# Attention and FFN on one core: the side work of the first FFN pass issued at other steps

## The chip, the cores and the metric

The kernel runs as one program on 1 core of one Trainium2 chip. The metric is the time of one execution in device microseconds (us). Below, PE is the matrix engine (TensorE), PEld its weight loads, DVE is VectorE, ACT is ScalarE, POOL is GpSimd and SP is SyncE, whose queue issues nearly all DMAs. Every engine works through its own queue in order and waits at an instruction whose inputs or buffers are not ready.

## The reference

```python
# attention: q, k, v are (4, 8, 768, 64)
mask = q_bucket[:, :, :, None] == k_bucket[:, :, None, :]
scores = np.where(mask, scale * q @ k.T, -1e9)
attn_out = softmax(scores) @ v
# FFN over x = (3072 tokens, 512)
h = x @ w_in                       # 512 x 2048
g = np.where(h >= 1, h, np.where(h <= -1, 0.0, (h + 1) ** 2 / 4))
return (g @ w_out).astype(np.float32)   # 2048 x 512
```

## The kernel before

The program has two phases: attention over 32 heads, then the FFN. Every float32 operand of a matrix product is split in two: a high part, rounded to the PE's fast format by a copy (a CAST in the trace), and a low part, the difference (a subtraction on line L39). A product of two such operands is three matmuls: high by high, high by low, low by high.

The FFN (`ffn`, L568) works through the 3072 tokens in 8 chunks of 384, and for each chunk through 16 tiles of 128 of the hidden dimension. One pair of chunk c and hidden tile f is a **step**. The loop at L669 runs over the steps in the order of `ffn_order`: steps 0 to 7 are (0,0) to (0,7), then chunk 1 and chunk 0 alternate ((1,0) is step 8, (0,8) step 9, and so on) until step 31; chunks 2 to 7 follow. This first pass over two chunks takes place while output weights and chunk 1's input are still being made.

A step issues in this order:

- the jobs of `prep[n]`, a table of what else is due at step n (L670);
- `g_lo` (L623): on DVE, the low part `glo` (L627) of the activation of the step before last;
- `gemm1` (L593): 12 matmuls (L600) into one of two PSUM buffers `h`: for each of the four input tiles ct = 0 to 3 high weight by high x, high weight by low x, low weight by high x. Low x of tile ct is so read by matmul 2, 5, 8 and 11. Then ACT makes `t` (L605) and `z` (L606), and DVE finishes the activation (L607, L608). L607 writes `t` in place, so it waits until L606 has read it;
- `g_hi` (L615): on ACT, the high part `ghi` (L620) of the step before;
- `gemm2` (L631) of three steps earlier (`GLAG` = 3): 9 matmuls (L638), for each of three token tiles `ghi` by high weight, `ghi` by low weight, `glo` by high weight.

So ACT and DVE have one queue each for the activations and for the jobs of `prep`, in the order in which the loop issues them. The jobs of the first pass are:

- **Chunk 1's input** (`xm.make`, L541, four tiles, four parts each): part 0 (L547) and part 1 (L550) on DVE scale the tile, part 2 (L552) rounds it on ACT, part 3 (L39) makes its low part on DVE. The tiles lie in buffers `xraw`, `xraw`, `xe`, `xr`.
- **Staged output weights**, hidden tiles 2 to 5: split earlier, parked in DRAM, and now fetched by a DMA (L102, `get`), rounded on ACT (L87, `s5`) and subtracted on DVE (L39, `s6`).
- **The other output weights**, hidden tiles 6 to 15: a DMA of the raw data (L62, `s0`), a square on ACT with a DVE operation (L69, L70, `s1`), DVE operations (L74, L78, L82, `s2` to `s4`), the rounding on ACT (L87, `s5`) and the subtraction on DVE (L39, `s6`).

`lsh_attn_ffn` sets the steps of the weights at L792 to L801. `need` is the step at which gemm2 first reads the tile; the numbers subtracted from it are the lead of s0 to s6. `wraw` and `wsq`, which these jobs fill, have two buffers each, so the DMA of a tile waits on SP until the tile two before it has been read.

```python
670  for fn, a in prep.pop(n, ()):
671      fn(*a)
672  g_lo()
673  pend.append((c, f, gemm1(c, f)))
674  g_hi(1)
675  if len(pend) > GLAG:
676      gemm2(*pend.pop(0))
```

Of the kernel before, what the change touches and what calls it, by code (L numbers as in the profile page):

```python
# [29 lines left out]
NFT = DFF // P  # L30
# [526 lines left out]
def ffn_order():  # L557


    steps = [(0, f) for f in range(LEAD)]  # L560
    for f in range(NFT):
        steps.append((1, f))
        if f + LEAD < NFT:
            steps.append((0, f + LEAD))
    return steps + [(c, f) for c in range(2, NCH) for f in range(NFT)]


def ffn(ctx, tc, wih, wil, woh, wol, xm, xa, xb, out, prep):  # L568
    nc = tc.nc
    xp = ctx.enter_context(tc.tile_pool(name="xp", bufs=1, reuse_waits="tile"))  # L570
    gp = ctx.enter_context(tc.tile_pool(name="gp", bufs=2, reuse_waits="tile"))
    ps_h = ctx.enter_context(tc.tile_pool(name="ps_h", bufs=2, space=PSUM, reuse_waits="tile"))
    ps_y = ctx.enter_context(tc.tile_pool(name="ps_y", bufs=6, space=PSUM, reuse_waits="tile"))
    mh = xp.tile([P, 1], F32, name="mh")
    nc.vector.memset(mh, 0.5)
    m1 = xp.tile([P, 1], F32, name="m1")
    nc.vector.memset(m1, -1.0)
    xc = (xp.tile([P, NCT, CH], F32R, name="xhi"), xp.tile([P, NCT, CH], F32R, name="xlo"))
    xs = [xa, xb] + [xc, xa] * ((NCH - 2) // 2)

    def piece(name):
        return xp.tile([P, CH], F32, name=name, bufs=2)

    def load_x(c, ct):
        if ct == 0:
            xm.load_sv(c, xp.tile([P, NCT, 2], F32, name="xsv"))
        if c == 1:
            xm.load_raw(c, ct, piece(("xraw", "xraw", "xe", "xr")[ct]))
        else:
            xm.load_raw(c, ct, piece("xraw"))  # L590
            xm.load_er(c, ct, piece("xe"), piece("xr"))

    def gemm1(c, f):  # L593
        hi, lo = xs[c]
        ps = ps_h.tile([P, 512], F32, name="h")
        n = 0
        for ct in range(NCT):
            cs = slice(ct * P, (ct + 1) * P)
            for w, x in ((wih[f], hi), (wih[f], lo), (wil[f], hi)):
                nc.tensor.matmul(out=ps[:, 0:CH], lhsT=w[:, cs], rhs=x[:, ct, :], start=(n == 0),  # L600
                                 stop=(n == 3 * NCT - 1))
                n += 1
        t = gp.tile([P, CH], F32, name="t")
        z = gp.tile([P, CH], F32, name="z", bufs=3)
        nc.scalar.activation(out=t, in_=ps[:, 0:CH], func=AF.Relu, scale=0.5, bias=mh)  # L605
        nc.scalar.activation(out=z, in_=t, func=AF.Relu, scale=1.0, bias=m1)  # L606
        nc.vector.scalar_tensor_tensor(out=t, in0=t, scalar=1.0, in1=t, op0=ALU.min, op1=ALU.mult)  # L607
        nc.vector.tensor_tensor(out=z, in0=t, in1=z, op=ALU.add)  # L608
        g = [None, None, z]
        to_hi.append(g)  # L610
        return g

    to_hi, to_lo = [], []

    def g_hi(left):  # L615

        while len(to_hi) > left:
            g = to_hi.pop(0)
            g[0] = gp.tile([P, CH], F32R, name="ghi", bufs=GLAG)
            nc.scalar.copy(out=g[0], in_=g[2])  # L620
            to_lo.append(g)

    def g_lo():  # L623
        while to_lo:
            g = to_lo.pop(0)
            g[1] = gp.tile([P, CH], F32R, name="glo", bufs=GLAG)
            nc.vector.tensor_tensor(out=g[1], in0=g[2], in1=g[0].bitcast(F32), op=ALU.subtract)  # L627

    ys = {}

    def gemm2(c, f, g):  # L631
        ghi, glo, _ = g
        if f == 0:
            ys[c] = [ps_y.tile([P, 512], F32, name="y") for _ in range(CH // P)]
        for m in range(CH // P):
            ms = slice(m * P, (m + 1) * P)
            for k, (g_, w) in enumerate(((ghi, woh[f]), (ghi, wol[f]), (glo, woh[f]))):
                nc.tensor.matmul(out=ys[c][m], lhsT=g_[:, ms], rhs=w, start=(f == 0 and k == 0),  # L638
                                 stop=(f == NFT - 1 and k == 2))
            if f == NFT - 1:  # L640
                r0 = c * CH + m * P
                if c == NCH - 1 and m == CH // P - 1:
                    for n, cp in ((0, nc.vector.tensor_copy), (1, nc.scalar.copy)):
                        cs = slice(n * DM // 2, (n + 1) * DM // 2)
                        ot = piece(("xraw", "xe")[n])[:, 0:DM // 2]
                        cp(out=ot, in_=ys[c][m][:, cs])
                        nc.sync.dma_start(out=out[r0:r0 + P, cs], in_=ot)
                    continue
                ot = xp.tile([P, DM], F32, name="ot", bufs=2)
                nc.scalar.copy(out=ot, in_=ys[c][m])  # L650
                nc.sync.dma_start(out=out[r0:r0 + P, :], in_=ot)

    def at(n, fn, *a):
        prep[n].append((fn, a))

    at(2 * NFT + 1, lambda: xm.sums_load(*(piece(n)[:, 0:NF] for n in ("xe", "xr")), B - 1))
    at(2 * NFT + 4, xm.sums_add)
    at(2 * NFT + 4, xm.sums_inv, B - 1)
    for ct in reversed(range(NCT)):
        prep[0].insert(0, (load_x, (1, ct)))  # L660
    for c in range(1, NCH):
        for ct in range(NCT):
            if c > 1:
                at((c - 1) * NFT + 4 + 2 * ct, load_x, c, ct)
            for part in range(4):
                n = (1, 2, 4, 5)[ct] + (0, 0, 1, 2)[part] if c == 1 else (c - 1) * NFT + 6 + 2 * ct + part
                at(n, xm.make, c, ct, part, *xs[c], [nc.vector if c == 1 else nc.gpsimd] * 2)
    pend = []
    for n, (c, f) in enumerate(ffn_order()):  # L669
        for fn, a in prep.pop(n, ()):  # L670
            fn(*a)
        g_lo()
        pend.append((c, f, gemm1(c, f)))
        g_hi(1)
        if len(pend) > GLAG:
            gemm2(*pend.pop(0))
    g_hi(0)
    g_lo()
    while pend:
        gemm2(*pend.pop(0))  # L680
# [3 lines left out]
def lsh_attn_ffn(ctx: ExitStack, tc: tile.TileContext, qk, v, pj, cv, w_in, w_out, out):  # L684
    nc = tc.nc
# [9 lines left out]
    NSTG = 10  # L695
    wih = [wp.tile([P, DM], F32R, name=f"wih{i}") for i in range(NW1)]
    wil = [wp.tile([P, DM], F32R, name=f"wil{i}") for i in range(NW1)]

    r_d = [xdp.tile([H, S], F32, name=f"rd{b}") for b in range(B)]
    xm = XMaker(nc, x_d, s_d, e_d, r_d)  # L700

    def flat(t):
        return t.rearrange("p a b s -> p (a b s)")
# [8 lines left out]
    for hi, lo in w0[0:4]:  # L712
# [3 lines left out]
    xa, xb = (tuple(flat(t)[:, n * NCT * CH:(n + 1) * NCT * CH].rearrange("p (c n) -> p c n", c=NCT)  # L716
                    for n in range(2)) for t in (T2[i0], T2[i1]))
# [3 lines left out]
    ws = WeightSplit(nc, wst, DM)  # L721

    tasks = defaultdict(list)
    prep = defaultdict(list)

    def at(g, fn, *a):
        tasks[g].append((fn, a))
# [8 lines left out]
    def wo_steps(i, cp, stage=None, low=None):  # L736
        return ws.steps(wout_v[i], (P, DM, 2), woh[i], wol[i], cp, stage, low)

    woh = [hi for hi, lo in wo]
    wol = [lo for hi, lo in wo]  # L740
# [3 lines left out]
    late = {}  # L744
    for n in range(NSTG):
        stage = xdp.tile([P, DM], F32, name=f"wd{n}")
        i = n - (NFT - NW1)
# [44 lines left out]
    for i in range(2, NFT):  # L792
        n = i + NFT - NW1
        need = i + GLAG if i < LEAD else 2 * i + GLAG + 1 - LEAD
        if n < NSTG:
            st = zip(late[n], (i - 4, i - 2, i - 1))
        else:
            st = zip(wo_steps(i, nc.scalar, None, nc.vector), (need - m for m in (9, 5, 5, 4, 4, 3, 2)))
        for fn, m in st:
            if m >= 0:  # L800
                prep[m].append((fn, ()))  # L801
    ffn(ctx, tc, wih, wil, woh, wol, xm, xa, xb, out, prep)


def _consts():
# [47 lines left out]
```

## Time and profile before

| what | value |
|---|---|
| median of 3 runs | 1021.6 us (1021.07 to 1022.53) |
| the profiled execution | 1021.61 us, span 1019.6 us |
| PE busy | 993.9 us, 97% of the span |
| DVE busy | 696.6 us, 68% |
| ACT busy | 647.5 us, 64% |
| POOL busy | 395.0 us, 39% |

The profile is of one execution. Its span runs from the first instruction to the last; the execution's own time is 2.0 us longer. Matmuls overlap, so the time from the start of one to the start of the next tells more than the duration of one. The FFN's first matmul starts at 473.54 us of the span.

### The profile page before, as it was taken

To read this page: it belongs to the slowest core of one execution; us is meant where nothing else is said; L and a number is where in the kernel's file an instruction comes from. 1 tells how busy PE (TensorE), PEld (TensorE's weight loads), DVE (VectorE), ACT (ScalarE), POOL (GpSimd) and SP (SyncE) were. 2 spreads that over 40 slices of the span, in tenths; PEclk is the share of its full clock that TensorE was granted. 3 is DMA by queue.
4 is the path that set the end of the run, shared out by engine and by line. 5 is a ranking of instruction groups with operands and counts; after the bars stand their busy time and mean duration, and the time that the engine had idled before them with its cause. 6 is when DMAs were issued, how large, how long until landed. Compare 5 with 4: busy or idle time off the path is not lost.

```text
span 1019.6 us, 15241 instructions
## 1 busy us (share of the span) xinstructions
PE 993.9 (97%) x5180; PEld 917.5 (90%) x5180; DVE 696.6 (68%) x1108; ACT 647.5 (64%) x1430; POOL 395.0 (39%) x458
## 2 busy tenths in 40 slices
PE   5899999999999999999999999999999999999998
PEld 4789999999999999989799999999999999999997
DVE  7678999999999998786977644544535445345332
ACT  5779888998899989886655444444444444444433
POOL 6666777777887777563000210201202102012000
PEclk9999999999999999999999999999999999999999
DMA  2645666766665655546222102102021021020000
GB/s 89 167 110 155 160 171 174 182 169 169 158 171 153 152 141 144 127 107 180 63 80 88 50 32 79 47 22 81 24 77 48 1 79 47 32 71 24 32 1 32
DMA packets 52229, 99.06 MB, mean 97 GB/s; under 512 B 12856, under 2 KB 33976, under 8 KB 52152
## 3 DMA queue, kind: packets, MB, share of 16 engines
q1 hardware_dynamic: 51936, 98.09, 35.9%
q8 instruction: 41, 0.67, 0.3%
q14 instruction: 36, 0.29, 0.1%
q10 hardware_dynamic: 216, 0.00, 0.0%
HBM read 57.38 MB, written 15.52 MB: 71 GB/s over the span
## 4 chain that ended last, share of the span: by engine, by line
PE 89%; DVE 5%; ACT 2%; DMA 1%; issue 1%; SPq 0%; POOL 0%; DVEq 0%; ACTq 0%
PE y L638 26%; PE h L600 25%; PE smax L258 7%; PE o L332 6%; PE s L298 6%; PE o L330 6%; PE o L331 6%; PE s L297 6%; PE o L178 2%; DVE nm L262 1%; DMA wsq<-wd 1%; DVE nm L359 1%; DVE pl L39 0%; ACT ph L306 0%; DMA pj_raw<-in_pj_dram 0%
## 5 line engine op out<-in xcount | busy, mean ns | idle before, releaser
L607 DVE SCALAR_TENSOR_TENSOR t<-t 128x384 f32<-128x384 f32 x128 | 73.0, 571 | 257.6 <-ACT z L606 257.5
L605 ACT ACTIVATE t<-h,mh 128x384 f32<-128x384 f32 x128 | 74.3, 581 | 267.4 <-PE h L600 266.2
L306 ACT ACTIVATE ph<-s 128x384 fp32r<-128x384 f32 x380 | 188.1, 495 | 46.9 <-PE s L298 40.6
L262 DVE TENSOR_REDUCE nm<-smax 128x1 f32<-128x768 f32 x186 | 176.2, 947 | 19.9 <-PE smax L258 18.4
L39 POOL TENSOR_TENSOR pl<-pf,ph 128x384 fp32r<-128x384 f32 x128 | 137.9, 1083 | 81.2 <-ACT pf L311 80.8
L39 DVE TENSOR_TENSOR pl<-s,ph 128x384 fp32r<-128x384 f32 x256 | 135.5, 544 | 15.3 <-ACT s L311 14.0
L550 POOL TENSOR_TENSOR xraw<-xraw,xr 128x384 f32<-128x384 f32 x24 | 30.2, 1258 | 272.2 <-DVE xraw L547 272.2
L297 PE MATMUL s<-t 128*128 128x384 f32 x384 | 132.0, 344 | 0.8 <-DVE t L212 0.8
L332 PE MATMUL o<-pl,va 128*128 128x386 f32 x384 | 130.4, 339 | 0.4 <-DVE pl L39 0.3
L298 PE MATMUL s<-t 128*128 128x384 f32 x384 | 130.2, 339 | 0.0
L330 PE MATMUL o<-ph,va 128*128 128x386 f32 x384 | 130.1, 339 | 0.0
L331 PE MATMUL o<-ph,vb 128*128 128x386 f32 x384 | 129.5, 337 | 0.0
L311 ACT ACTIVATE s<-s 128x384 f32<-128x384 f32 x252 | 125.3, 497 | 0.0
L600 PE MATMUL h<-t,wih 128*128 128x384 f32 x480 | 122.7, 336 | 0.0
L638 PE MATMUL y<-t,ghi 128*128 128x512 f32 x384 | 120.2, 394 | 0.0
L258 PE MATMUL smax<-t 128*128 128x384 f32 x372 | 101.5, 353 | 5.4 <-DVE nm L262 4.5
L600 PEld LDWEIGHTS h<-t,wih 128*128 128x128 f32 x480 | 88.0, 188 | 4.9
L258 PEld LDWEIGHTS smax<-t 128*128 128x128 f32 x372 | 63.9, 188 | 22.1 <-DVE nm L262 21.1
L606 ACT ACTIVATE z<-t,m 128x384 f32<-128x384 f32 x128 | 79.0, 617 | 4.1
L638 PEld LDWEIGHTS y<-t,ghi 128*128 128x128 f32 x384 | 71.4, 188 | 11.2
L600 PE MATMUL h<-t,wil 128*128 128x384 f32 x240 | 80.8, 337 | 0.0
L638 PE MATMUL y<-t,glo 128*128 128x512 f32 x192 | 76.3, 398 | 2.9 <-DVE glo L627 2.9
(130 smaller groups left out, 2117.2 us busy)
## 6 DMA issues: line engine op xcount, KB each, us to landing
t<-t SPq DMA_DIRECT2D x60, 384.0 KB
raw<-in_qk_dram SPq DMA_DIRECT2D x15, 768.0 KB
wraw<-in_w_in_dram SPq DMA_DIRECT2D x16, 512.0 KB
wraw<-in_w_out_dram SPq DMA_DIRECT2D x16, 512.0 KB
xd<-xs SPq DMA_DIRECT2D x32, 192.5 KB
vraw<-in_v_dram SPq DMA_DIRECT2D x16, 384.0 KB
out_dram<-ot SPq DMA_DIRECT2D x23, 256.0 KB
xraw<-xd SPq DMA_DIRECT2D x26, 192.0 KB
```

What stands on the lines that cost most here:

```text
L39: eng.tensor_tensor(out=out, in0=a, in1=b, op=ALU.subtract)
L258: nc.tensor.matmul(out=smax[hd][:, hf, 0:HS], lhsT=t2[:, 0, h, i * P:(i + 1) * P], rhs=t2[:, 1, h, hf * HS:(hf + 1) * HS], start=True, sto ...
L262: nc.vector.tensor_reduce(out=nmp(hd)[:, i:i + 1], in_=smax[hd][:, :, 0:HS], axis=AX.XY, op=ALU.max, negate=True)
L297: nc.tensor.matmul(out=ps[:, 0:HS], lhsT=t1[:, 1, h, ks], rhs=t1[:, 0, h, sl], start=True, stop=False)
L298: nc.tensor.matmul(out=ps[:, 0:HS], lhsT=t2[:, 1, h, ks], rhs=t2[:, 0, h, sl], start=False, stop=True)
L306: nc.scalar.activation(out=ph[:, 0:HS], in_=ps[:, 0:HS], func=AF.Exp, scale=SCALE)
L311: nc.scalar.activation(out=pf, in_=ps[:, 0:HS], func=AF.Exp, scale=SCALE)
L330: nc.tensor.matmul(out=o, lhsT=wa, rhs=ph, start=(jj == 0), stop=False)
L331: nc.tensor.matmul(out=o, lhsT=wb, rhs=ph, start=False, stop=False)
L332: nc.tensor.matmul(out=o, lhsT=wa, rhs=pl, start=False, stop=(jj == NJ - 1))
L600: nc.tensor.matmul(out=ps[:, 0:CH], lhsT=w[:, cs], rhs=x[:, ct, :], start=(n == 0), stop=(n == 3 * NCT - 1))
L638: nc.tensor.matmul(out=ys[c][m], lhsT=g_[:, ms], rhs=w, start=(f == 0 and k == 0), stop=(f == NFT - 1 and k == 2))
```

## The change

The change edits only when jobs of the first pass are issued. A second table, `post`, holds jobs that are issued after g_hi, so behind the step's activations, and before gemm2. `g_lo` now comes ahead of the jobs of `prep`. Chunk 1's input is made one step later, its rounding (part 2) in `post` of the same step as parts 0 and 1, its low part two steps after. The roundings of all output weights go to `post`. The staged tiles 2 to 5 are fetched, rounded and subtracted later (tiles 2 and 3 were fetched during attention and still are); tiles 6 to 15 get their steps s1 to s5 one step later or in `post`, and from tile 8 on their DMA three steps later.

```diff
     pend = []
     for n, (c, f) in enumerate(ffn_order()):
+        g_lo()
         for fn, a in prep.pop(n, ()):
             fn(*a)
-        g_lo()
         pend.append((c, f, gemm1(c, f)))
         g_hi(1)
+        for fn, a in post.pop(n, ()):
+            fn(*a)
         if len(pend) > GLAG:
             gemm2(*pend.pop(0))
...
             for part in range(4):
-                n = (1, 2, 4, 5)[ct] + (0, 0, 1, 2)[part] if c == 1 else (c - 1) * NFT + 6 + 2 * ct + part
-                at(n, xm.make, c, ct, part, *xs[c], [nc.vector if c == 1 else nc.gpsimd] * 2)
+                if c == 1:
+                    n = (2, 3, 5, 6)[ct] + (0, 0, 0, 2)[part]
+                    (post if part == 2 else prep)[n].append((xm.make, (c, ct, part, *xs[c], [nc.vector] * 2)))
+                else:
+                    at((c - 1) * NFT + 6 + 2 * ct + part, xm.make, c, ct, part, *xs[c], [nc.gpsimd] * 2)
...
         if n < NSTG:
-            st = zip(late[n], (i - 4, i - 2, i - 1))
+            st = zip(late[n], (i - 1, i - (i < 4), i + 1))
         else:
-            st = zip(wo_steps(i, nc.scalar, None, nc.vector), (need - m for m in (9, 5, 5, 4, 4, 3, 2)))
-        for fn, m in st:
-            if m >= 0:
+            st = zip(wo_steps(i, nc.scalar, None, nc.vector), (need - m for m in (9 if i < 8 else 6, 4, 4, 3, 3, 3, 2)))
+        *st, (cast, m_cast), low = st
+        post[m_cast].append((cast, ()))
+        for fn, m in st + [low]:
+            if n >= NSTG or i > 3 or fn is low[0]:
                 prep[m].append((fn, ()))
```

The instructions are the same, in another order on DVE, ACT and SP. PE's order is the same.

DVE from L608 of step 0 on, before (names are result <- inputs; `t1_0_74<-wsq` are the low parts of output weights 2 and 3, `xraw` is chunk 1's input, tiles 0 and 1):

```order
L608 TENSOR_TENSOR z_6069<-t_6068,z_6069 128x384
L39 TENSOR_TENSOR t1_0_74<-wsq_5929,t1_0_74 128x512
L547 SCALAR_TENSOR_TENSOR xraw_6042<-t2_2_79,xsv_6040,xraw_6042 128x384
L550 TENSOR_TENSOR xraw_6042<-xraw_6042,t2_2_79 128x384
L607 SCALAR_TENSOR_TENSOR t_6095<-t_6095 128x384
L608 TENSOR_TENSOR z_6096<-t_6095,z_6096 128x384
L39 TENSOR_TENSOR t1_0_74<-wsq_5949,t1_0_74 128x512
L547 SCALAR_TENSOR_TENSOR xraw_6044<-t2_2_79,xsv_6040,xraw_6044 128x384
L550 TENSOR_TENSOR xraw_6044<-xraw_6044,t2_2_79 128x384
L627 TENSOR_TENSOR glo_6108<-z_6069,ghi_6101 128x384
```

and with the change:

```order
L608 TENSOR_TENSOR z_6066<-t_6065,z_6066 128x384
L607 SCALAR_TENSOR_TENSOR t_6086<-t_6086 128x384
L608 TENSOR_TENSOR z_6087<-t_6086,z_6087 128x384
L627 TENSOR_TENSOR glo_6095<-z_6066,ghi_6092 128x384
L547 SCALAR_TENSOR_TENSOR xraw_6042<-t2_2_79,xsv_6040,xraw_6042 128x384
L550 TENSOR_TENSOR xraw_6042<-xraw_6042,t2_2_79 128x384
L607 SCALAR_TENSOR_TENSOR t_6112<-t_6112 128x384
L608 TENSOR_TENSOR z_6113<-t_6112,z_6113 128x384
L627 TENSOR_TENSOR glo_6122<-z_6087,ghi_6118 128x384
L39 TENSOR_TENSOR t1_0_74<-wsq_5929,t1_0_74 128x512
```

The first `glo` stood behind six jobs and one more activation; now it stands behind one activation.

DVE before, from L607 of step 6 on (`t2_0_77<-wsq` are the low parts of output weights 6 and 7, `t2_2_79<-xr` is the low part of chunk 1's tile 3, which matmul 11 of step 8 reads; `wa` is a step of output weight 8):

```order
L607 SCALAR_TENSOR_TENSOR t_6277<-t_6277 128x384
L608 TENSOR_TENSOR z_6278<-t_6277,z_6278 128x384
L39 TENSOR_TENSOR t2_0_77<-wsq_6173,t2_0_77 128x512
L70 TENSOR_SCALAR wa_6297<-wraw_6133 128x512
L74 SCALAR_TENSOR_TENSOR wa_6297<-wraw_6133,wsc_111,wa_6297 128x512
L39 TENSOR_TENSOR t2_2_79<-xr_6048,t2_2_79 128x384
L627 TENSOR_TENSOR glo_6304<-z_6241,ghi_6283 128x384
L607 SCALAR_TENSOR_TENSOR t_6319<-t_6319 128x384
L608 TENSOR_TENSOR z_6320<-t_6319,z_6320 128x384
L39 TENSOR_TENSOR t2_0_77<-wsq_6215,t2_0_77 128x512
```

and with the change, from L39 of tile 2 (`xe`) on; the L607 here is step 7's:

```order
L39 TENSOR_TENSOR t2_2_79<-xe_6046,t2_2_79 128x384
L607 SCALAR_TENSOR_TENSOR t_6308<-t_6308 128x384
L608 TENSOR_TENSOR z_6309<-t_6308,z_6309 128x384
L627 TENSOR_TENSOR glo_6326<-z_6271,ghi_6314 128x384
L39 TENSOR_TENSOR t2_0_77<-wsq_6248,t2_0_77 128x512
L70 TENSOR_SCALAR wa_6330<-wraw_6253 128x512
L74 SCALAR_TENSOR_TENSOR wa_6330<-wraw_6253,wsc_111,wa_6330 128x512
L39 TENSOR_TENSOR t2_2_79<-xr_6048,t2_2_79 128x384
L607 SCALAR_TENSOR_TENSOR t_6350<-t_6350 128x384
```

The low part of tile 3 stood ahead of L607 and L608 of step 7; now it stands behind them, behind one more pair of `glo`, and behind output weight 7's subtraction.

ACT, from the last copy of attention on, before (`t1_0_74<-wsq` and `t2_0_77<-wsq` are the roundings of output weights 2, 3, 4 and 5):

```order
L338 COPY xs_5961<-o1_143 128x386
L87 CAST t1_0_74<-wsq_5929 128x512
L605 ACTIVATE t_6068<-h_6055,mh_6034 128x384
L606 ACTIVATE z_6069<-t_6068,m1_6036 128x384
L87 CAST t1_0_74<-wsq_5949 128x512
L605 ACTIVATE t_6095<-h_6082,mh_6034 128x384
L606 ACTIVATE z_6096<-t_6095,m1_6036 128x384
L620 CAST ghi_6101<-z_6069 128x384
L87 CAST t1_0_74<-wsq_6051 128x512
L552 CAST t2_2_79<-xraw_6042 128x384
L605 ACTIVATE t_6123<-h_6110,mh_6034 128x384
```

and with the change:

```order
L338 COPY xs_5961<-o1_143 128x386
L605 ACTIVATE t_6065<-h_6052,mh_6034 128x384
L606 ACTIVATE z_6066<-t_6065,m1_6036 128x384
L605 ACTIVATE t_6086<-h_6073,mh_6034 128x384
L606 ACTIVATE z_6087<-t_6086,m1_6036 128x384
L620 CAST ghi_6092<-z_6066 128x384
L87 CAST t1_0_74<-wsq_5929 128x512
L605 ACTIVATE t_6112<-h_6099,mh_6034 128x384
L606 ACTIVATE z_6113<-t_6112,m1_6036 128x384
L620 CAST ghi_6118<-z_6087 128x384
L87 CAST t1_0_74<-wsq_5949 128x512
L552 CAST t2_2_79<-xraw_6042 128x384
```

The activations of steps 1 and 2 now stand ahead of the roundings of weights 2 and 3; that of weight 4, whose data come by a DMA issued in this pass, moved from ahead of step 2's activation to behind step 4's.

## Rows read from the trace of the kernel before

**Rows 1.** The page's first part: busy time of each engine.

```profile
PE 993.9 (97%) x5180; PEld 917.5 (90%) x5180; DVE 696.6 (68%) x1108; ACT 647.5 (64%) x1430; POOL 395.0 (39%) x458
```

**Rows 2.** Waits in the FFN, engine and line, for whom: total us, times, longest.

```profile
PEld y L638 <- DVE glo L627: 4.7, 4, 1.3
...
PE y L638 <- DVE glo L627: 2.9, 4, 0.9
```

**Rows 3.** PE in order of time: start us, us, engine, line, operation, [idle before].

```profile
481.89 0.63 PE L638 MATMUL y<-t,ghi 128*128 128x512 f32 x2
...
498.81 0.50 PE L638 MATMUL y<-t,glo 128*128 128x512 f32 x1 [0.82 <-DVE glo L627]
...
502.64 0.62 PE L638 MATMUL y<-t,ghi 128*128 128x512 f32 x2
...
505.80 0.51 PE L600 MATMUL h<-t,wih 128*128 128x384 f32 x2
...
506.32 0.51 PE L600 MATMUL h<-t,wih 128*128 128x384 f32 x2
506.67 0.34 PE L600 MATMUL h<-t,wil 128*128 128x384 f32 x1
506.84 0.62 PE L638 MATMUL y<-t,ghi 128*128 128x512 f32 x2
```

**Rows 4.** DVE in order of time, in the FFN's first pass.

```profile
477.24 0.56 DVE L607 SCALAR_TENSOR_TENSOR t<-t 128x384 f32<-128x384 f32 x1 [4.62 <-ACT z L606]
...
489.61 0.68 DVE L39 TENSOR_TENSOR t<-wsq,t 128x512 fp32r<-128x512 f32 x1
490.21 0.42 DVE L70 TENSOR_SCALAR wa<-wraw 128x512 int32<-128x512 int32 x1
490.66 0.75 DVE L74 SCALAR_TENSOR_TENSOR wa<-wraw,wsc,wa 128x512 int32<-128x512 int32 x1
491.33 0.55 DVE L39 TENSOR_TENSOR t<-xraw,t 128x384 fp32r<-128x384 f32 x1
491.81 0.61 DVE L547 SCALAR_TENSOR_TENSOR xe<-t,xsv,xe 128x384 f32<-128x384 f32 x1
492.45 0.56 DVE L550 TENSOR_TENSOR xe<-xe,t 128x384 f32<-128x384 f32 x1
492.93 0.55 DVE L627 TENSOR_TENSOR glo<-z,ghi 128x384 fp32r<-128x384 f32 x1
493.39 0.55 DVE L607 SCALAR_TENSOR_TENSOR t<-t 128x384 f32<-128x384 f32 x1
493.98 0.56 DVE L608 TENSOR_TENSOR z<-t,z 128x384 f32<-128x384 f32 x1
494.45 0.74 DVE L78 SCALAR_TENSOR_TENSOR wa<-wraw,wsc,wa 128x512 int32<-128x512 int32 x1
495.23 0.69 DVE L82 SCALAR_TENSOR_TENSOR wsq<-wsq,wa 128x512 f32<-128x512 f32 x1
495.96 0.43 DVE L70 TENSOR_SCALAR wa<-wraw 128x512 int32<-128x512 int32 x1
```

**Rows 5.** ACT in order of time: the activation of step 1, the rounding of weight 4.

```profile
478.54 0.62 ACT L606 ACTIVATE z<-t,m 128x384 f32<-128x384 f32 x1
...
483.35 0.62 ACT L87 CAST t<-wsq 128x512 fp32r<-128x512 f32 x1 [3.79 <-DMA wsq<-wd]
```

**Rows 6.** SP's DMA issues in order of time: the fetch of weight 4.

```profile
479.05 0.32 SPq L102 DMA_DIRECT2D wsq<-wd  x1
```

**Rows 7.** Engines in one stretch: busy us (instructions), PE clock granted, DMA share, GB/s.

```profile
480.00:482.00 2.00, 2.00 (x13) 2.00 (x12) 1.97 (x5) 0.00 (x0) 0.00 (x0) 1.00 0.94 292
```

**Rows 8.** PE in order of time, at the start of the kernel.

```profile
12.06 0.66 PE L356 MATMUL s<-t 128*128 128x384 f32 x1 [2.42 <-DVE t L212]
...
17.39 0.39 PE L356 MATMUL s<-t 128*128 128x384 f32 x1
```

**Rows 9.** Engines in one stretch, as rows 7: the end, behind the last matmul.

```profile
1015.80:1019.60 3.80, 0.01 (x1) 0.00 (x0) 0.42 (x1) 0.37 (x1) 0.00 (x0) 1.00 0.55 207
```

More of the change, by code (lines that the diff above doesn't have):

```diff
@@ L565, in ffn_order, with ffn @@
     return steps + [(c, f) for c in range(2, NCH) for f in range(NFT)]
-def ffn(ctx, tc, wih, wil, woh, wol, xm, xa, xb, out, prep):
+def ffn(ctx, tc, wih, wil, woh, wol, xm, xa, xb, out, prep, post):
     nc = tc.nc
@@ L723, in lsh_attn_ffn @@
     tasks = defaultdict(list)
-    prep = defaultdict(list)
+    prep, post = defaultdict(list), defaultdict(list)
     def at(g, fn, *a):
@@ L795, in lsh_attn_ffn @@
         if n < NSTG:
-            st = zip(late[n], (i - 4, i - 2, i - 1))
+            st = zip(late[n], (i - 1, i - (i < 4), i + 1))
         else:
-            st = zip(wo_steps(i, nc.scalar, None, nc.vector), (need - m for m in (9, 5, 5, 4, 4, 3, 2)))
-        for fn, m in st:
-            if m >= 0:
+            st = zip(wo_steps(i, nc.scalar, None, nc.vector), (need - m for m in (9 if i < 8 else 6, 4, 4, 3, 3, 3, 2)))
[3 more added lines that the diff above has]
+            if n >= NSTG or i > 3 or fn is low[0]:
                 prep[m].append((fn, ()))
-    ffn(ctx, tc, wih, wil, woh, wol, xm, xa, xb, out, prep)
+    ffn(ctx, tc, wih, wil, woh, wol, xm, xa, xb, out, prep, post)
 def _consts():
```

## The prediction

> **What bounds the kernel now.** I read the page first, to see which engine has no room: PE is busy 97% of the span [rows 1], so only what makes PE wait can give time back. The waits of the FFN come next: PE waits there for one thing alone, `glo` from DVE, four times on the matmul and four times on its weight load, 1.3 us at the longest [rows 2]. Then I read PE in order of time around these waits. gemm2 of step 3 starts at 481.89 and gemm2 of step 7 at 502.64, after the last of the four waits (498.81) [rows 3]. That is 20.75 us for four steps. The next step, without a wait, takes 506.84 - 502.64 = 4.20 us, four such 16.80. **PE loses 3.95 us here**, and nowhere else in the first pass. This is all that the change can win.
>
> Why is `glo` late? DVE in order of time shows it: from 489.61 to 495.96 one operation starts as soon as the one before lets it, weight jobs, input jobs and activations in one queue, and `glo` stands behind the jobs [rows 4]. DVE, not PE, sets the pace of these steps. The reader should see two things in this stretch: a late `glo` is the symptom, the amount of DVE work before a due date is the cause.
>
> **The change, part by part.** No instruction is added or taken away, so what counts is who stands ahead of whom.
>
> *The glo ahead of the jobs.* The first four `glo` come early. From the spacings of rows 4 (start to start): L607 and L608 together 0.59 + 0.47 = 1.06 us, `glo` 0.46, a weight's subtraction 0.60, L547 and L550 0.64 + 0.48 = 1.12, an input's low part 0.48, L70 and L74 0.45 + 0.67 = 1.12, L78 and L82 0.78 + 0.73 = 1.51. DVE starts L607 of step 0 at 477.24 [rows 4] and is through with that pair at 478.30. L607 of step 1 waits for ACT's `z`, which ends at 478.54 + 0.62 = 479.16 [rows 5]. Then, in the order of the changed queue, `glo` of step 2 starts at 479.16 + 3 x 1.06 + 2 x 0.46 + 0.60 + 2 x 1.12 = 486.10 and takes 0.55; it is due on PE at 481.89 + 2 x 4.20 = 490.29. `glo` of step 3 starts at 487.64 (the turn of step 4's pair, below) + 1.06 = 488.70, and is due at 494.49. So the four waits go: minus 3.95 us, if nothing else is late.
>
> *What is late next: chunk 1's input.* Its tiles are made a step later, and the low part of tile 3 now stands behind L607 and L608 of step 7. DVE's queue up to it holds, counted in the changed order: 8 pairs L607 and L608 (8.48), 7 `glo` (3.22), 6 weight subtractions (3.60), 4 pairs L547 and L550 (4.48), 3 pairs L70 and L74 (3.36), 2 pairs L78 and L82 (3.02), three low parts (1.44) and the last one at its full 0.55. The sum is 28.15 us. With the start at 477.24 and one idle of 479.16 - 478.30 = 0.86, the last low part ends at 477.24 + 0.86 + 28.15 = **506.25**. Who waits for it: matmul 11 of step 8. Before, that matmul started midway between 506.32 and 506.67, at 506.50 [rows 3]. Without the 3.95 it would want to start at 502.55. So PE waits **3.70 us** there, and gains 3.95 - 3.70 = **0.25 us** in all. Part of the wait comes at matmul 8, which would be ready at 505.97 - 3.95 = 502.02 and finds tile 2's low part done at 502.5; then three matmuls run and PE stands still some 3.1 us, until 506.25. Behind that nothing of the first pass is late: DVE has caught up, `glo` of steps 5 and 6 lie before the low part in its queue, and step 9's matmuls find all they need.
>
> Whether DVE itself is held up on the way: L607 of step 4 comes up at 479.16 + 3 x 1.06 + 3 x 0.46 + 2 x 0.60 + 2 x 1.12 + 0.48 = 487.64. PE ends step 4's gemm1 at about 486.09 + 0.17, and two ACT operations of about 0.62 [rows 5] give 487.5. It is met with 0.1 to spare; every later one with more, since PE would run ahead of DVE by then.
>
> *The fetch of staged weight 4.* It is issued when weight 2's subtraction has read its buffer, at 479.16 + 2 x 1.06 + 2 x 0.46 + 1.12 + 0.68 = 484.0, not at 479.05 [rows 6]. Before, its rounding could start 4.3 us after the issue (483.35 [rows 5]), ACT idle 3.79 of it with step 2's activation queued behind. Now 484.0 + 4.3 + 0.62 = 488.9, and the subtraction's turn on DVE is 487.64 + 1.06 + 0.46 = 489.16: hidden, by 0.25. Two raw tiles of 512 KB each now stand ahead of it in the DMA queue. At 292 GB/s [rows 7] one is 1.8 us. The bounds are 0 and, with one tile still ahead, 1.8 - 0.25 = 1.55 us, all of it on DVE's chain. I take 0: the issue comes 4.95 us later, in which the queue moves 1.4 MB, more than the 1.05 MB added.
>
> *The raw weights.* From tile 8 on the DMA comes at need - 6, when L78 of the tile two before (step need - 7) has freed its buffer. Two steps, 8.4 us, are left until L70 reads it, against 4.3 for a landing: nothing. If that cover were gone, L70 would hold up DVE, and with it `glo`. Chunk 2's loads stand behind the last raw tile on SP; it comes at step 20, and their first reader is step 22, again 8.4 us. The roundings behind g_hi are off the path, with one use two steps on. POOL's queue isn't touched.
>
> **The sum**: 1021.61 (the profiled execution, equal to the median of 1021.6) - 0.25 = 1021.4 us. Hand-overs between engines, which I have not counted, eat some of it. The 51 spacings in the sum, each off by 0.01, make 0.5 either way.
>
> **Rivals.** What a measurement of this kernel can tell from no change is 0.2%, 2.0 us: under 1019.6 is faster, over 1023.6 slower.
>
> 1. *The waits go and none takes their place*: 1021.6 - 3.95 = 1017.7. For it: PE's waits name `glo` alone [rows 2], and half of a step's reads of chunk 1's low parts come late in gemm1. Against it: DVE would have to be through 28 us of work 3.7 us sooner, and rows 4 show no idle to take them from. Chance 0.06.
>
> 2. *The one longer stop costs PE its clock.* Four stops of about 1 us become one of about 3. At the start of the kernel PE runs at the lower of its levels (1.2 GHz): the same matmul takes 0.66 us at 12.06 and 0.39 at 17.39 [rows 8]. If the clock fell in the stop of step 8 and took as long to come back, 5.3 us, PE would lose half of that, 2.7: 1021.4 + 2.7 = 1024.1, slower. It decides from the length of stop at which the clock falls; the FFN has none over 1.3 us [rows 2] to tell. Against it: at the end of the span 3.80 us pass with no matmul started and the granted clock is still 1.00 [rows 9], and the stop here is shorter. Chance 0.09. The Trainium skill ("TensorE: Matmul & The Clock Gate", Part 1: The HAM clock gate) calls the throttled clock the default state, to which an idle TensorE goes back; by that rule alone this rival's 1024.1 would be the time. The trace shows it for the start of the kernel and doesn't show it for a stop of 3 us.
>
> 3. *Weight 4 lands late*: up to 1.55 us more on DVE, 1021.4 + 1.55 = 1022.95, and 1.8 more if both raw tiles were ahead. Chance 0.07, of which 0.02 over the bound.
>
> 4. *The change does not do what it says*, and `glo` stays late: 1021.6 again. The slack of 4.2 and 5.8 us worked out above leaves it no room; it lies within the forecast's range.
>
> **How the numbers follow.** The forecast, an exchange of one wait for another, has 0.78. Its own range is 1020.6 to 1022.2 (spacings 0.5, hand-overs 0.3). Rival 3 adds 0.07 and carries the range to 1023.0; rivals 1 and 2, together 0.15, are left out. Faster: rival 1 and 0.01 for a misread chain, 0.07. Slower: rival 2 and 0.02 of rival 3, 0.11. The same: 0.82.
>
> **What would show it.** Right: no PE wait for `glo`; two waits of PE h L600 for a DVE L39, about 0.5 and 3.1 us, between 502 and 506.3; DVE without a gap from 479.2 to 506.3, L607 of step 7 starting at about 502.5; ACT's wait of 3.79 for the DMA gone; matmuls at full clock after the stop; from step 9 on a step of 4.20. Wrong: L600 without a wait at 502; a DVE idle before a weight's subtraction near 489 with a DMA behind it; a granted clock under 1.00 after 506.

## The result and the profile after

The change made the kernel **slower**: 1023.22 us median (1021.59 to 1026.73, 20 runs) against 1020.54 (1019.44 to 1023.21, 20 runs), ratio 1.0024 with a 95% interval of 1.0017 to 1.0031. The ratio stands for 2.4 us, the two medians differ by 2.7. The median lies beyond the range that was given (1020.6 to 1023.0) on the side that had a chance of 0.11. The profiled execution took 1024.03 us, its span 1022.1 us.

The waits of PE in the FFN come first (who waited for whom: total us, times, longest), in the kernel after, as in [rows 2]:

```profile
PEld h L600 <- DVE t L39: 4.0, 2, 3.2
PE h L600 <- DVE t L39: 3.3, 2, 2.9
```

No `glo` is left in them. In its place stand two waits of gemm1 for a subtraction on L39: the low parts of chunk 1's tiles 2 and 3. PE in order of time shows where, in the kernel after (start, us, engine, line, operation, [idle before]):

```profile
500.53 0.51 PE L600 MATMUL h<-t,wih 128*128 128x384 f32 x2
...
502.31 0.44 PE L600 MATMUL h<-t,wih 128*128 128x384 f32 x1 [0.37 <-DVE t L39]
...
502.77 0.33 PE L600 MATMUL h<-t,wih 128*128 128x384 f32 x1
506.04 0.69 PE L600 MATMUL h<-t,wih 128*128 128x384 f32 x1 [2.93 <-DVE t L39]
...
506.84 1.05 PE L638 MATMUL y<-t,ghi 128*128 128x512 f32 x2
...
510.68 0.84 PE L600 MATMUL h<-t,wih 128*128 128x384 f32 x2
...
513.28 0.62 PE L638 MATMUL y<-t,ghi 128*128 128x512 f32 x2
...
517.48 0.62 PE L638 MATMUL y<-t,ghi 128*128 128x512 f32 x2
```

Step 8 starts at 500.53, waits 0.37 us at matmul 8 and 2.93 us at matmul 11. What follows is new: the pair of matmuls at 506.84 takes 1.05 us where the same pair at 513.28 takes 0.62, and gemm2 of step 8 lasts 510.68 - 506.84 = 3.84 us instead of about 2.1. The granted clock says why. Engines by stretches of 2 us, kernel after (columns: PE, PEld, DVE, ACT, POOL busy, the granted clock as a share of 2.4 GHz, DMA share, GB/s):

```profile
502.00:504.00 2.00, 0.79 (x3) 0.47 (x3) 1.97 (x5) 1.02 (x2) 0.00 (x0) 1.00 0.71 262
504.00:506.00 2.00, 0.00 (x0) 0.00 (x0) 1.95 (x4) 0.00 (x0) 0.00 (x0) 0.74 0.00 0
506.00:508.00 2.00, 1.96 (x5) 1.77 (x6) 0.00 (x0) 0.89 (x2) 0.00 (x0) 0.50 0.00 0
508.00:510.00 2.00, 2.00 (x6) 1.52 (x6) 1.62 (x4) 0.71 (x2) 0.00 (x0) 0.50 0.00 0
510.00:512.00 2.00, 2.00 (x8) 1.81 (x7) 1.31 (x2) 0.00 (x0) 0.00 (x0) 0.56 0.17 45
512.00:514.00 2.00, 2.00 (x13) 1.87 (x12) 0.00 (x0) 0.52 (x1) 0.00 (x0) 1.00 0.63 217
```

PE starts no matmul between 504 and 506, the clock falls to 0.50, that is 1.2 GHz, and stays there until shortly before 512, although PE is busy all the time from 506.04 on. Column and durations agree here. They do not everywhere: for the kernel before the column reads 1.00 from 0 to 20 us, where the matmuls of [rows 8] go from 0.66 to 0.39 us, so that the lower level at the start is read from the durations alone.

The attention phase does not start the FFN at the same point in every execution, so the FFN is best compared by itself: from the start of its first matmul to the start of its last. Before, that is 1015.42 - 473.54 = 541.88 us; after, 1017.65 - 473.29 = 544.36. **The FFN alone is 2.48 us longer.** Each such figure is of one profiled execution. The mean clock of the 20 timed runs of the kernel after was between 0.994 and 0.998 in every one.

DVE in order of time, kernel after, at its first idle and from L607 of step 7 on:

```profile
478.95 0.56 DVE L607 SCALAR_TENSOR_TENSOR t<-t 128x384 f32<-128x384 f32 x1 [0.81 <-ACT z L606]
...
502.18 0.55 DVE L607 SCALAR_TENSOR_TENSOR t<-t 128x384 f32<-128x384 f32 x1
502.76 0.56 DVE L608 TENSOR_TENSOR z<-t,z 128x384 f32<-128x384 f32 x1
503.24 0.55 DVE L627 TENSOR_TENSOR glo<-z,ghi 128x384 fp32r<-128x384 f32 x1
503.71 0.68 DVE L39 TENSOR_TENSOR t<-wsq,t 128x512 fp32r<-128x512 f32 x1
504.31 0.42 DVE L70 TENSOR_SCALAR wa<-wraw 128x512 int32<-128x512 int32 x1
504.76 0.75 DVE L74 SCALAR_TENSOR_TENSOR wa<-wraw,wsc,wa 128x512 int32<-128x512 int32 x1
505.43 0.55 DVE L39 TENSOR_TENSOR t<-xr,t 128x384 fp32r<-128x384 f32 x1
508.34 0.56 DVE L607 SCALAR_TENSOR_TENSOR t<-t 128x384 f32<-128x384 f32 x1 [2.36 <-ACT z L606]
```

Between 478.95 and 505.98 DVE has no idle. The low part of tile 3 ends at 505.43 + 0.55 = 505.98, in an FFN that starts 0.25 us earlier than the one before. DVE, which kept four `glo` late [rows 4], now keeps two low parts late, in all by nearly as much.

### The profile page after: what moved, and what is told of

Read it like the earlier page. It is cut to its first block, busy times and chain, and to the rows that moved or that the text cites. A ratio compares the mean times of both kernels' runs of the same rounds, so it can differ in the third digit from the quotient of the medians.

```text
span 1022.1 us, 15230 instructions
## 1 busy us (share of the span) xinstructions
PE 996.5 (97%) x5180; PEld 920.0 (90%) x5180; DVE 696.7 (68%) x1108; ACT 647.8 (63%) x1430; POOL 390.1 (38%) x458
## 4 chain that ended last, share of the span: by engine, by line
PE 89%; DVE 5%; ACT 2%; DMA 2%; issue 1%; SPq 0%; POOL 0%; DVEq 0%; ACTq 0%
PE y L638 25%; PE h L600 25%; PE smax L258 7%; PE s L298 6%; PE o L332 6%; PE o L330 6%; PE o L331 6%; PE s L297 6%; PE o L178 2%; DVE nm L262 1%; DMA t<-te 1%; DVE nm L359 1%; DVE t L39 1%; PE o L276 0%; DVE glo L627 0%
## 5 line engine op out<-in xcount | busy, mean ns | idle before, releaser
L607 DVE SCALAR_TENSOR_TENSOR t<-t 128x384 f32<-128x384 f32 x128 | 72.5, 567 | 258.9 <-ACT z L606 258.9
L39 POOL TENSOR_TENSOR pl<-pf,ph 128x384 fp32r<-128x384 f32 x128 | 138.7, 1089 | 81.2 <-ACT pf L311 80.9
L39 DVE TENSOR_TENSOR pl<-s,ph 128x384 fp32r<-128x384 f32 x256 | 135.6, 544 | 15.8 <-ACT s L311 14.9
L550 POOL TENSOR_TENSOR xraw<-xraw,xr 128x384 f32<-128x384 f32 x24 | 24.7, 1028 | 286.1 <-DVE xraw L547 286.1
L600 PE MATMUL h<-t,wih 128*128 128x384 f32 x480 | 124.0, 338 | 3.3 <-DVE t L39 3.3
L600 PEld LDWEIGHTS h<-t,wih 128*128 128x128 f32 x480 | 88.7, 189 | 8.9 <-DVE t L39 4.0
L627 DVE TENSOR_TENSOR glo<-z,ghi 128x384 fp32r<-128x384 f32 x128 | 89.3, 698 | 0.2 <-ACT ghi L620 0.2
L600 PE MATMUL h<-t,wil 128*128 128x384 f32 x240 | 81.2, 338 | 0.0
```

Source lines behind the costliest of these rows:

```text
L39: eng.tensor_tensor(out=out, in0=a, in1=b, op=ALU.subtract)
```

## The experiments

Two theories of the loss stood at the start. Theory A: DVE's work ahead of a due date sets PE's stop, the change turned four stops into one long one, and the loss is the clock that falls in it. Rival B: the new order costs time of itself. Each ratio below is to the kernel before on the same chip; "FFN" is the span from first to last matmul of the profiled execution, to be set against 541.88.

**Fill the stop.** 12 useless matmuls ahead of matmul 11 of step 8:

```diff
+                if c == 1 and f == 0 and n == 10:
+                    ys[1] = [ps_y.tile([P, 512], F32, name="y") for _ in range(CH // P)]
+                    for _ in range(12):
+                        nc.tensor.matmul(out=ys[1][0], lhsT=wih[0][:, 0:P], rhs=woh[0], start=True, stop=True)
...
-        if f == 0:
+        if c not in ys:
             ys[c] = [ps_y.tile([P, 512], F32, name="y") for _ in range(CH // P)]
```

> The changed kernel with 12 extra matmuls (512 columns, about 0.23 us apart, 2.8 us) ahead of matmul 11 of step 8, into a PSUM bank not yet in use; their results are overwritten. Theory A (the long stop for tile 3's low part lets the clock fall, and the low clock is the loss): PE stays at 1.00, step 9 takes 4.2 us and the time is about 2.5 us under the changed kernel, at 1020.3 to 1020.7, the same as before. Rival B (the new order costs PE time whatever the clock does): it stays at 1023.

Measured: 1021.34 us, over the expected 1020.3 to 1020.7, but the kernel before took 1020.92 beside it: ratio 1.0003 (0.9994 to 1.0011); FFN 541.76, 0.12 less than before. PE in order of time (the new lines make L604 of L600; L603 are the 12):

```profile
502.85 2.91 PE L603 MATMUL y<-t,wih 128*128 128x512 f32 x12
505.95 0.44 PE L604 MATMUL h<-t,wih 128*128 128x384 f32 x1 [0.19 <-DVE t L39]
```

and the two stretches that had 0.74 and 0.50:

```profile
504.00:506.00 2.00, 1.81 (x9) 1.18 (x7) 1.86 (x4) 0.00 (x0) 0.00 (x0) 1.00 0.00 0
506.00:508.00 2.00, 2.00 (x9) 1.72 (x10) 0.14 (x1) 1.37 (x3) 0.00 (x0) 1.00 0.00 0
```

Matmul 11 starts no earlier (505.95 against 506.04) and DVE does the same work. Only the clock is kept, and the whole loss is gone. Rival B falls. The 0.12 is also the first direct measure of the exchange of waits, for which 0.25 was forecast.

**Half of the fill**, `range(6)`:

> The changed kernel with 6 extra matmuls instead of 12 ahead of matmul 11 of step 8 (1.4 us), so that about 1.6 us of the stop are left. Theory A with the length of the stop deciding: the clock stays at 1.00, time as with 12 of them, within 0.1% of before. Rival E (any stop over 1 us at this place lets the clock fall): a fall behind step 8 and a time about 0.2% over before.

Measured: 1021.37 us, ratio 1.0003 (0.9994 to 1.0012); FFN 541.80. PE idles 1.55 us ahead of matmul 11; no run had a mean clock under 0.999. Rival E falls for a stop of that length.

**Tile 3's low part one step earlier:**

```diff
-                    n = (2, 3, 5, 6)[ct] + (0, 0, 0, 2)[part]
+                    n = (2, 3, 5, 6)[ct] + (0, 0, 0, 2 if ct < 3 else 1)[part]
```

> The changed kernel with only the low part of chunk 1's tile 3 made one step earlier, so that on DVE it stands ahead of L607 and L608 of step 7, one glo, weight 7's subtraction and L70 and L74 (3.25 us). Theory A: it ends at 502.7 instead of 506.0, PE waits about 0.5 us in step 8 in all, the clock stays at 1.00, and the time is before minus 3.95 plus 0.5, 1017.1 (ratio to before 0.9966). Rival C (whatever is put behind it, glo or weight 7, is late in its place): PE waits for a glo or for weight 7 in steps 8 to 10 and the time stays over 1019.

Measured: 1018.08 us, ratio 0.9974 (0.9965 to 0.9983); FFN 538.57, 3.31 less than before; the only PE wait in the FFN is 0.4 us at matmul 8. One entry of the table separates a loss of 2.5 us from a gain of 3.3. Rival C falls: PE waits for no `glo` and no weight in their place.

**The same, and weight 7's last steps one step later:**

```diff
-... for m in (9 if i < 8 else 6, 4, 4, 3, 3, 3, 2))
+... for m in ((9, 4, 4, 2, 2, 2, 1) if i == 7 else (9 if i < 8 else 6, 4, 4, 3, 3, 3, 2)))
```

> As the kernel with the earlier low part of tile 3, and output weight 7's L78, L82, rounding and subtraction one step later as well. Theory A: DVE has 1.4 us less ahead of both low parts, PE has no wait left in the first pass, time before minus 3.95, 1016.6 (ratio 0.9961). Rival C: weight 7, now one step closer to its use at step 10, or the fetch of raw weight 9, whose buffer it frees, is late: a wait of PE for L638 at step 10 and a time over 1018.

Measured: 1018.12 us, ratio 0.9974 (0.9964 to 0.9983); FFN 537.91, 3.97 less than before, with no PE wait. The FFN's gain is as expected, to 0.02 us. PE waits for no weight either, so rival C falls, although the time is over the 1018 that it had named. The time is not as expected: it is no shorter than with the low part alone. Two of the 9 runs had a mean clock of 0.997 and 0.998, although no stop is left in the FFN; where it fell in those the profile, which is of another run, can't show.

**Only the glo ahead**, in the kernel before:

```diff
+        g_lo()
         for fn, a in prep.pop(n, ()):
             fn(*a)
-        g_lo()
```

> The kernel before with only the glo ahead of the step's jobs. Theory A: DVE has the same work and one glo more ahead of tile 3's low part (ending about 505.9 instead of 505.4), so PE wins at the glo waits and stops for that low part in step 8 instead, about 2.8 us in one piece; if the clock falls there as in the changed kernel, time 1022 to 1023, if not 1020. Rival D (a glo behind the jobs was the cause of the four waits, and what else moved in the change made the loss): no stop in step 8, time 1017 to 1018.

Measured: 1021.83 us, ratio 1.0011 (1.0002 to 1.002); FFN 1017.17 - 476.20 = 540.97, 0.91 less than before. PE in the FFN waits once for ACT and once for tile 3's low part:

```profile
487.53 0.62 PE L600 MATMUL h<-t,wih 128*128 128x384 f32 x2 [0.72 <-ACT t L605]
...
508.16 0.45 PE L600 MATMUL h<-t,wih 128*128 128x384 f32 x1 [1.79 <-DVE t L39]
```

Rival D falls: without any of the later steps, a stop in step 8 already takes the place of the four waits, with a smaller one ahead of it. Theory A had the size wrong, 2.8 us expected and 1.79 measured: ACT still waited 3.74 us for weight 4's DMA, so that PE lost 0.72 us before it came to step 8, and the low part of tile 3 ended no later, counted from the FFN's first matmul, than in the kernel before, where 0.5 more was expected. In this execution the clock held in the FFN and fell elsewhere: between 60 and 70 us, in attention, behind a PE wait of 1.4 us for a DMA:

```profile
PE s L298 <- DMA t<-te: 1.4, 1, 1.4
```

```profile
60.00:65.00 5.00, 3.39 (x15) 2.75 (x15) 2.94 (x5) 1.75 (x4) 2.45 (x5) 0.88 0.10 19
65.00:70.00 5.00, 5.00 (x25) 4.93 (x24) 2.51 (x4) 3.42 (x9) 4.76 (x7) 0.78 0.00 0
```

Six of 11 runs had a mean clock of 0.998 or less, this one among them; where it fell in the other five isn't shown.

**Weight 8's first operations later.** This and the next change the stop's length through the order alone:

```diff
-... for m in (9 if i < 8 else 6, 4, 4, 3, 3, 3, 2))
+... for m in (9 if i < 8 else 6, *((3, 3) if i == 8 else (4, 4)), 3, 3, 3, 2))
```

> The changed kernel with weight 8's L69, L70 and L74 one step later, so behind tile 3's low part on DVE. Theory A: that low part ends 1.12 us sooner, at about 504.9; the stop at matmul 11 shrinks from about 3.0 to 1.9 us, the clock stays at 1.00, and the FFN takes 1.4 us less than before (1019.5, ratio 0.9987). Rival E (a stop of 2 us is already enough): the clock falls, ratio over 1.001.

Measured: 1020.45 us, ratio 1.0001 (0.9991 to 1.0011); FFN 540.65, 1.23 less than before; PE idles 1.81 us. The profiled execution kept its clock and took 1019.38 us. The runs split in two: six with a mean clock of 0.999 or 1.000 took 1019.38 to 1020.45 us, five with 0.994 to 0.998 took 1021.54 to 1023.5. So neither side had it right: theory A's clock did not hold in every run, and the median is not over 1.001 as rival E had it. No profile shows where the clock fell in the five.

**Only L74 of weight 8 later**, `4, 3 if i == 8 else 4, 3, 3, 3, 2`:

> The changed kernel with only L74 of weight 8 one step later (0.67 us): the stop at matmul 11 of step 8 lies between that of the changed kernel (2.93 us idle, a mean clock of 0.998 or less in 20 of 20 runs) and that with L69, L70 and L74 later (1.8 us, 5 of 11 runs), at about 2.3 us. Theory A with the length of the stop deciding: a low mean clock in more than half of the runs and fewer than all, the FFN 0.9 us shorter than before in runs without a fall, median 1021 to 1023. Rival E (it is chance, whatever the length): no order by length.

Measured: 1021.61 us, ratio 1.001 (1.0001 to 1.0019). The stop, and the stretches behind it:

```profile
504.66 0.44 PE L600 MATMUL h<-t,wih 128*128 128x384 f32 x1 [2.15 <-DVE t L39]
```

```profile
504.00:506.00 2.00, 1.34 (x4) 1.20 (x5) 0.60 (x2) 0.56 (x1) 0.00 (x0) 0.75 0.00 0
506.00:508.00 2.00, 2.00 (x6) 1.55 (x5) 1.27 (x3) 1.04 (x3) 0.00 (x0) 0.50 0.00 0
508.00:510.00 2.00, 2.00 (x11) 1.81 (x11) 1.93 (x4) 0.00 (x0) 0.00 (x0) 0.90 0.00 0
```

Here the fall came 0.3 us behind the start of matmul 11 and lasted 3.4 us, half as long as the 6.8 us of the kernel after, of which 1.1 lay in the stop. The FFN is 542.52, 0.64 longer than before where 0.9 shorter was due without the fall: it cost about 1.5 us. Eight of 11 runs had a mean clock of 0.998 or less (1021.42 to 1023.72 us), three had 1.000 (1019.88 to 1020.68). This is as expected.

**The stop without the change.** The kernel before, its low part of tile 3 one step later:

```diff
-                n = (1, 2, 4, 5)[ct] + (0, 0, 1, 2)[part] if c == 1 else (c - 1) * NFT + 6 + 2 * ct + part
+                n = (1, 2, 4, 5)[ct] + (0, 0, 1, 2 + ct // 3)[part] if c == 1 else (c - 1) * NFT + 6 + 2 * ct + part
```

> The kernel before, with nothing of the change, but the low part of chunk 1's tile 3 one step later, so behind step 7's activation, weight 7's subtraction and weight 8's L78 and L82. It ends at about 508.9 instead of 505.4. Theory A: the four waits for glo stay, PE stops a fifth time, at matmul 11 of step 8, for about 2.4 us, and in a part of the runs the clock falls there: time 1023.4 in runs without a fall and 1025 to 1026.5 in runs with one (ratio 1.0025 to 1.005). Rival G (the clock falls only in the changed order, not through a stop as such): all runs near 1023.4.

Measured: 1024.81 us, ratio 1.0036 (1.0022 to 1.0049); FFN 543.64, 1.76 longer than before. The profiled execution kept its clock and took 1021.97 us; the four others had a mean clock of 0.998 and took 1024.55 to 1026.49. PE idled 2.68 us:

```profile
506.74 0.45 PE L600 MATMUL h<-t,wih 128*128 128x384 f32 x1 [2.68 <-DVE t L39]
```

Rival G falls by the count, four runs of 5 against 2 of 68 of the kernel before: a stop here costs the clock in the old order too. The place of the fall in those four isn't shown, since the profiled one kept its clock. The FFN was 1.76 longer and not 2.4, since one of the four waits for `glo` went; the rest of the 1.4 us by which the profiled run was under the expected 1023.4 lies outside the FFN, which began at 472.13 and not at 473.54.

**Chunk 1's input at the steps of before**, the rest as changed:

```diff
-                    n = (2, 3, 5, 6)[ct] + (0, 0, 0, 2)[part]
-                    (post if part == 2 else prep)[n].append((xm.make, (c, ct, part, *xs[c], [nc.vector] * 2)))
+                    n = (1, 2, 4, 5)[ct] + (0, 0, 1, 2)[part]
+                    prep[n].append((xm.make, (c, ct, part, *xs[c], [nc.vector] * 2)))
```

> The changed kernel with chunk 1's input made at the steps of before (all four parts in the first table); glo ahead, weights as changed. Theory A (of the change it is the input's later steps alone that cost): tile 3's low part stands where it stood, ahead of step 7's activation, the first scaling fills DVE's 0.8 us idle, PE has no wait in the first pass, and the FFN takes 3.95 us less than before (1017.0, ratio 0.9961). Rival F (the weights' later steps matter as much): PE still waits over 1 us in steps 3 to 10, ratio over 0.998.

Measured: 1017.9 us, ratio 0.997 (0.9957 to 0.9982); FFN 538.26, 3.62 less than before; the one wait left is of a weight load, 0.4 us, at matmul 11 of step 8. Rival F falls: of the change, the input's later steps alone turn the gain into a loss.

**Both improvements**, input at the old steps and weight 7 later:

> The changed kernel with chunk 1's input at the steps of before, and weight 7's L78, L82, rounding and subtraction one step later: the two versions that won, together. Theory A: tile 3's low part ends 1.4 us before PE wants it, PE has no wait in the first pass, FFN 3.95 us shorter than before, no fall of the clock; 1017.0 (ratio 0.9962), no faster than each of the two by more than 0.4 us since only that much wait was left.

Measured: 1017.61 us, ratio 0.9965 (0.9952 to 0.9979); FFN 1010.73 - 472.80 = 537.93, 3.95 less than before, no PE wait. This version beats both kernels. It had the lowest median of all, though the intervals of the four winners overlap.

Ordered by PE's idle ahead of matmul 11 in the profiled execution, the runs with a mean clock of 0.998 or less. A fall behind the last matmul costs no time and can by itself bring the mean to 0.999 (2.5 us at 0.50 at the end of the span, in the profile with weight 8's L69, L70, L74 later), so the count starts at 0.998:

| kernel | idle, us | runs at 0.998 or less |
|---|---|---|
| both improvements; low part earlier; input at old steps | 0 to 0.4 | 0 of 5; 0 of 11; 0 of 6 |
| low part earlier and weight 7 later | 0 | 2 of 9 |
| 12 extra matmuls | 0.19 | 0 of 11 |
| 6 extra matmuls | 1.55 | 0 of 11 |
| only the glo ahead | 1.79 | 6 of 11 |
| weight 8's L69, L70, L74 later | 1.81 | 5 of 11 |
| weight 8's L74 later | 2.15 | 8 of 11 |
| before, with the low part later | 2.68 | 4 of 5 |
| after | 2.93 | 20 of 20 |

Of the 68 runs of the kernel before beside these, 2 had such a clock, so a few falls come from elsewhere. The table counts runs by their mean clock and gives the idle time of one of them. A fall in step 8 itself was seen in the two profiles with 2.15 and 2.93 us; those with 1.79, 1.81 and 2.68 us kept their clock there. That the other runs fell there too is argued from the counts. By them the last rival E, chance whatever the length, falls: in the main the share of low runs grows with the stop from 1.55 us on. Why one run falls and another of the same kernel does not stays open.

## Why the prediction was wrong

*The loss of the four waits for glo*: right. They went, and a first pass without any wait is 3.95 us shorter, as worked out: 3.95 and 3.97 were measured where nothing took their place.

*What is late next*: right, to within 0.2 us. Forecast were a DVE without idle from 479.2, L607 of step 7 at about 502.5, stops of 0.5 and 3.1 us, and 0.25 us won in all. Measured were no idle from 478.95, L607 at 502.18 (with an FFN that starts 0.25 us earlier), 0.37 and 2.93 us, and 0.12 us won where the clock was kept.

*The fetch of weight 4*: right, it cost nothing. Its rounding on ACT, which had waited 3.79 us [rows 5], started without a wait; so did the subtraction on DVE at 488.99, between two operations back to back.

*The raw weights*: right, no wait for one in steps 9 and on; a step takes 517.48 - 513.28 = 4.20 us again.

*The clock*: this is the step that failed. The sum put the one longer stop at its 3.7 us of waiting and its effect on the clock at nothing. That effect was the prediction's rival 2, with the right place, the right price for the profiled execution (2.7 us worked out; 2.48 + 0.25 = 2.7 measured against the forecast, 2.6 against the 0.12 really won) and **a chance of 0.09** for what the mean clocks then showed in 20 of 20 runs. In the price there is some luck. It was taken from 5.3 us of slow matmuls at the start of one execution; in the twelve profiles that start lasts from 5.3 to about 6.9 us, and the fall with L74 later cost 1.5. The argument against it was [rows 9]: at the end of the span 3.80 us pass at 1.00. That was one execution. The same stretch in the profile of the version with both improvements:

```profile
1011.20:1013.20 2.00, 0.00 (x0) 0.00 (x0) 0.42 (x1) 0.37 (x1) 0.00 (x0) 1.00 0.94 351
1013.20:1015.70 2.50, 0.00 (x0) 0.00 (x0) 0.00 (x0) 0.00 (x0) 0.00 (x0) 0.66 0.12 36
```

After the last matmul, started at 1010.73, the clock is at 1.00 for 2 us and then falls, well within 4 us. Of the twelve profiles seven fall like this, 2.4 to 3.3 us after the start of the last matmul, that of the kernel after among them; five keep 1.00 to the end of the span, for 4.2 to 4.8 us. No matmul tests the column there. One tail that keeps its clock shows only that the clock need not fall in that time. From it I took that it does not. The sentence of the Trainium skill ("TensorE: Matmul & The Clock Gate", Part 1: The HAM clock gate) that stood beside the rival, that an idle TensorE goes back to the throttled clock, is what the granted 0.50 behind the stop shows. Taken alone, as the prediction took it, it would have every stop cost the clock, and the 11 runs with 1.55 us show no fall. The same section says of a kernel's start that the number of matmuls run at the low clock varies from run to run of one kernel. The traces agree, by the durations: of the twelve matmuls of L356 [rows 8], in a part of the program that is the same in all the kernels here, 8 to 12 take 0.63 us or more. Behind the stop the length varies too: the mean clocks of the 20 runs of the kernel after spread from 0.994 to 0.998.

So the forecast's exchange of one wait for another was right as far as it went, and its sum lacked a term: the price of having the wait in one piece.

## What to carry to other kernels

PE's idle time is not one sum: four waits of 0.4 to 0.9 us cost 3.95 us; the stops of 0.37 and 2.93 us in their place cost 3.83 and then 2.6 more, for the clock. So when a change gathers small waits into one, look for the length of the longest stop that is left, and let no single quiet stretch of one execution speak against a fall. When the engine that feeds the due dates has no idle, look which operation moved behind which due date: here one table entry, a subtraction of 0.5 us placed behind 3.3 us of less urgent work, decided between 0.24% lost and 0.26% won.

## What was not expected of the hardware

The mean clock was low in about half of the runs of the two kernels with a stop of only 1.8 us, in none of 11 with 1.55, in 8 of 11 with 2.15 and in all 20 with 2.93. That is no threshold: in attention one profile shows a fall behind a wait of 1.4 us, and another keeps its clock behind 2.68. That one and the same program gives both was the surprise; it makes a kernel's times spread in two groups, 1019.4 to 1020.5 and 1021.5 to 1023.5 us for the stop of 1.81.

Twelve matmuls whose results nobody reads cost nothing in a stop and saved 2.6 us of FFN time after it.

Two things stay open. The FFN's first matmul started between 472.00 and 476.20 us in the profiled executions, although the attention phase is the same program. The 476.20 is that of the execution with the fall in attention; why the others spread up to 473.92 was not tried. And the timed gain of the version with the low part earlier and weight 7 later (0.26%, 2.7 us) is less than the 3.97 us that its FFN won in the profile. In the profiles 1.1 us of the difference lies outside the FFN: it started 0.4 us later, and the span ended 4.9 us after the start of the last matmul, against 4.2 in the kernel before. Why is open; falls of the clock in two of its 9 runs account for a part at most.
